# Masks of a third head group on TensorE, q and k of the second batch in four half-transfers, and a new order of steps

## The chip, the cores and the metric

The kernel runs on one core of one Trainium2 chip. Times are device microseconds of that core, one launch. A core has five engines with queues of their own: TensorE (PE; its weight loads are listed as PEld), VectorE (DVE), ScalarE (ACT), GpSimd (POOL) and SyncE (SP), and 16 DMA engines that the queues share. Matmul results land in eight banks of PSUM; a bank is free for the next matmul once another engine has read it.

## The reference

```python
# q, k, v: (8, 8, 576, 64); window 32
scores = (q @ k.T) / sqrt(64);  scores = where(|i - j| <= 32, scores, -1e9)
attn = softmax(scores);  a = attn @ v
x = a.transpose(0, 2, 1, 3).reshape(4608, 512)
# mixture of experts, 8 experts, top 1, w1 (8, 512, 1024), w2 (8, 1024, 512)
logits = x @ w_gate + modality_bias[modality_id]
e = argmax(logits);  gate = softmax(logits)[e]
out = gate * (relu(x @ w1[e]) @ w2[e])
```

## The kernel before, in words

The whole program is one list of steps written out by hand, the string ORDER. A step is a name with numbers, then the engine it goes to (`/v` DVE, `/a` ACT, `/p` POOL), or the PSUM banks it writes (`:0123`). A loop at the end of the function calls the function of each step in turn, and every engine runs its own instructions in that order; waits between engines come from the data. So the order of the list is the order of each engine's queue, and a step that waits holds up all that stands behind it on its engine.

Attention, per batch b (8) and head group g (2 per batch, four heads each; group number 2b + g):
- `l.b.u.g` loads q (u = 0) or k (u = 1) of batch b through POOL's DMA queue, cast to bf16; g = 2 takes both groups in one transfer (576 KB), g = 0 or 1 one group (288 KB). `lv.b.i` loads a half of v (288 KB).
- `t.b.g.u` transposes one of them on DVE into the layout for the scores.
- `SA`, `SB` are the score matmuls of a group in two parts, four banks each; `sa`, `sb` the exps on ACT into the tile pt (sa is one instruction, sb two).
- The band mask is applied in one of two ways. For groups listed in `PM`, `MA` and `MB` first write a table of 0 and a huge negative number into the banks (4 matmuls of 384 columns; MB has 4 of 128 columns more), and the scores add to it. For the others, `M.it` multiplies pt by a 0/1 mask on DVE, two steps of two heads for a group; `it` runs over 32 pairs of heads, so group 2 has M4 and M5.
- `V.it` is the product with v (18 matmuls, two banks), `v.it` the division by the sum and the write to x_t on DVE (a reciprocal, then one product).

Dispatch: `s0` to `s16` make, from the modality ids, each token's place in one list that holds the tokens of one modality from the front and those of the other from the back. `G.b` is a one-hot on DVE, `X.b.m` moves and transposes tokens with it on PE, `pa` and `pb` copy the result on ACT into XT. `Jo`, `Je` and `Jm` make the list of row numbers in the same way. `e` steps find the expert of each modality and the gate weights.

Experts: `W1.i` and `W2.i` load the weights of the expert of list end i (1024 KB each, POOL's queue). `U.t.mp` is 8 matmuls of 256 columns (a quarter of the first layer for 256 tokens, tile t), `u` the relu on ACT or DVE, `D.t.s.hf` 4 matmuls of 512 columns of the second layer, `y.t.s` the product with the gate weight, `O.t.s` the scatter of 128 rows to the output by POOL. Tile 18 is a short tile across the middle of the list. `L`, `lo`, `E`, `sm`, `rc` are the gate. `n2` and `n4` are fillers: 2 or 4 matmuls of 256 columns on zeros, whose result nobody reads. `K` steps make constants: Kw0 the zeros, Kw1 and Kw2 ones, Kn the table of the mask, Kb the 0/1 mask, Kq, Kp and Ko the padding of tiles, Kc others. Steps `c` check assumptions of this path; a general path stands behind an If at the end and is not run.

Steps around the change: U0.0 is the first expert matmul. It needs W1.0, `pa0.0` to `pa0.4`, and a free bank. The first D step needs W2.0.

## Time and profile before

| what | value |
|---|---|
| median of 3 runs | 209.55 us (209.44 to 210.11) |
| the profiled execution | 209.1 us, its span 207.5 us |
| PE, DVE, ACT, POOL busy | 194.9, 149.9, 133.0, 98.9 us |
| fillers on PE | 88 matmuls, 13.1 us busy |
| mean granted clock of TensorE | 0.996 of full speed |

The span is from the first to the last instruction; what the execution took beyond it (1.6 us) lies around the program. Busy times of matmuls overlap in the pipeline, so time per matmul is better read from the start of one group to the start of the next.

### The profile page before, as it was taken

To read this page: it belongs to the slowest core of one execution; us is meant where nothing else is said; L and a number is where in the kernel's file an instruction comes from. 1 tells how busy PE (TensorE), PEld (TensorE's weight loads), DVE (VectorE), ACT (ScalarE), POOL (GpSimd) and SP (SyncE) were. 2 spreads that over 40 slices of the span, in tenths; PEclk is the share of its full clock that TensorE was granted. 3 is DMA by queue.
4 is the path that set the end of the run, shared out by engine and by line. 5 is a ranking of instruction groups with operands and counts; after the bars stand their busy time and mean duration, and the time that the engine had idled before them with its cause. 6 is when DMAs were issued, how large, how long until landed. Compare 5 with 4: busy or idle time off the path is not lost. (4 is left out here: it accounts for less than half of the span.)

```text
span 207.5 us, 6240 instructions
## 1 busy us (share of the span) xinstructions
PE 194.9 (94%) x2585; PEld 139.8 (67%) x2585; DVE 149.9 (72%) x293; ACT 133.0 (64%) x226; POOL 98.9 (48%) x143
## 2 busy tenths in 40 slices
...
PEclk9999999999999999999999999999999999999998
...
GB/s 67 202 174 185 211 209 193 212 193 212 200 186 234 169 211 213 206 115 206 186 171 68 97 175 0 83 128 113 51 102 53 332 128 54 103 101 51 54 158 57
DMA packets 47629, 30.41 MB, mean 147 GB/s; under 512 B 38851, under 2 KB 38891, under 8 KB 47339
## 3 DMA queue, kind: packets, MB, share of 16 engines
...
## 5 line engine op out<-in xcount | busy, mean ns | idle before, releaser
L961 POOL DMA_INDIRECT out_dram<-ys,ids x37 | 40.6, 1098 | 87.2 <-ACT ys L952 33.8
L916 PE MATMUL banks<-XT,w_sb 128*128 128x256 bf16 x576 | 71.4, 273 | 0.3 <-DVE xt L758 0.3
L942 PE MATMUL banks<-w_sb,hT 128*128 128x512 bf16 x288 | 69.8, 379 | 0.0
L916 PEld LDWEIGHTS <-w_sb 128*128 128x128 bf16 x576 | 53.8, 98 | 10.9 <-issue 1.3
L695 ACT ACTIVATE pt<-banks 128x1536 bf16<-128x1536 f32 x32 | 46.4, 1453 | 14.0 <-PE banks L687 9.5
L933 ACT ACTIVATE hT<-banks 128x512 bf16<-128x512 f32 x57 | 33.0, 600 | 30.0 <-PE banks L916 27.5
L942 PEld LDWEIGHTS <-hT 128*128 128x128 bf16 x296 | 26.7, 98 | 25.6 <-issue 0.6
L655 DVE STREAM_TRANSPOSE qk<-qk 128x576 int32<-128x576 int32 x32 | 38.5, 1244 | 1.8 <-DMA qk<-in_q_dram 1.1
L712 DVE TENSOR_TENSOR pt<-pt,mask 128x1920 bf16<-128x1920 bf16 x28 | 32.1, 1169 | 3.5 <-ACT pt L695 3.4
L758 DVE TENSOR_TENSOR xt<-banks,recs 128x640 bf16<-128x640 f32 x32 | 26.4, 824 | 1.2
L729 PEld LDWEIGHTS <-pt 128*128 128x128 bf16 x576 | 21.2, 97 | 3.6 <-issue 0.4
L729 PE MATMUL banks<-vt,pt 128*128 128x65 bf16 x576 | 22.7, 193 | 0.4 <-DVE pt L712 0.2
L931 DVE TENSOR_SCALAR hT<-banks 128x512 bf16<-128x512 f32 x17 | 11.5, 685 | 15.9 <-PE banks L916 15.9
L952 ACT ACTIVATE ys<-banks,Gt 128x512 f32<-128x512 f32 x20 | 13.7, 691 | 12.9 <-PE banks L942 12.1
L798 ACT CAST XT<-banks 128x352 f32 (+3 forms) x40 | 18.0, 449 | 5.7 <-PE banks L778 4.9
L687 PE MATMUL banks<-qk 32*128 32x192 bf16 (+1 forms) x640 | 18.8, 239 | 2.5 <-DVE oh_ab L613 1.6
L231 POOL DMA_DIRECT2D vt<-in_v_dram x16 | 20.5, 1285 | 0.2 <-issue 0.2
L954 DVE TENSOR_SCALAR ys<-banks,Gt 128x512 f32<-128x512 f32 x17 | 12.7, 744 | 10.3 <-PE banks L942 4.7
L812 ACT CAST XT<-banks 128x352 f32 (+2 forms) x39 | 17.6, 452 | 1.9 <-PE banks L778 1.3
L687 PEld LDWEIGHTS <-qk 32*128 32x128 bf16 x640 | 12.3, 93 | 9.6 <-issue 6.8
L970 PE MATMUL banks<-zero_b 128*128 128x256 bf16 x88 | 13.1, 297 | 1.8 <-POOL zero_b L320 1.3
L778 PEld LDWEIGHTS <-xt 128*128 128x128 bf16 x160 | 10.5, 98 | 4.9 <-issue 0.8
...
## 6 DMA issues: line engine op xcount, KB each, us to landing
vt<-in_v_dram POOLq DMA_DIRECT2D x16, 288.0 KB
w_sb<-in_moe_w_dram POOLq DMA_DIRECT2D x4, 1024.0 KB
...
wx<-w_sb SPq DMA_DIRECT2D x2, 1024.0 KB, 6.2
out_dram<-ys,ids POOLq DMA_INDIRECT x37
qk<-in_k_dram POOLq DMA_DIRECT2D x2, 288.0 KB
qk<-in_q_dram POOLq DMA_DIRECT2D x2, 288.0 KB
```

Of the source, the lines that this page charges most:

```text
L231: nc.gpsimd.dma_start(v_t[b % NV][:, n_ * i:n_ * i + n_, 0:D], v[b].rearrange("h s d -> (h s) d").rearrange("(n p) d -> p n d", p=P)[:, n_ ...
L655: nc.vector.transpose(qk_t[b % 2][:, g, at:at + S].rearrange("p (t r) -> p r t", r=R), Ct["l", b][:, u, g].bitcast(I32).rearrange("p (r j) ...
L687: nc.tensor.matmul(st[:, h, WIN * i_:WIN * i_ + w_], qk[32 * h:32 * h + 32, c_, QK + k0:QK + k0 + P], qk[32 * h:32 * h + 32, c_, q0:q0 + w ...
L695: nc.scalar.activation(pt[:, :, 2 * part:2 * part + 2, 0:WIN], st[:, :, 0:2 * WIN].rearrange("p h (j c) -> p h j c", c=WIN), ACT.Exp, scal ...
L712: nc.vector.tensor_tensor(out=p_ap, in0=p_ap, in1=mask[:], op=ALU.mult)
L729: nc.tensor.matmul(o_ap, pt[:, c1:c1 + P], vt[:, g0 + j, 0:D + 1], start=(m == 0 and i_ == 0), stop=(i_ == len(mine) - 1), skip_group_chec ...
L758: nc.vector.tensor_tensor(out=o_ap, in0=o_v[:, :, :, 0:D], in1=rec.unsqueeze(3).to_broadcast([P, 2, NM, D]), op=ALU.mult)
L798: ins = nc.scalar.copy(XT[:, :, bass.ds(r_, w_)], Ct["X", b, m][:, :, 0:w_])
L916: ins = nc.tensor.matmul(ph[:, u_, :], w1[:, f0:f0 + 2 * P - 1:2], rhs, start=(kd == 0), stop=(kd == n_kd - 1))
L933: nc.scalar.activation(o_ap, i_ap, ACT.Relu)
L942: nc.tensor.matmul(Ct["D", t_, s_], Ct["h", t_][:, kf, P * s_:P * s_ + P], w2, start=(kf == 0), stop=(kf == n_kf - 1))
L961: ins = nc.gpsimd.indirect_dma_start(out=out, out_offset=bass.IndirectOffsetOnAxis(ap=ids[:, u_:u_ + 1], axis=0), in_=Ct["y", t_, s_][:], ...
```

## The change

- `PM` becomes (0,1,2): group 2, the first of batch 1, gets `MB1.0` and `MA1.0` on PE; `M4` and `M5` on DVE go.
- q and k of batch 1 come in four transfers of one group each, in the order k of group 0, q of group 0, then after v of batch 0 q of group 1, v's first half of batch 1, and k of group 1, instead of one transfer of q and, later, one of k.
- The order is new throughout. Steps change engine: Kw0, Kw1, Kw2, Kq1, s0, e9, Je1.2, Je7.2 go to DVE; Kv and e5 to POOL; relu and output steps are exchanged between ACT and DVE (u on DVE 19 instead of 17, y 16 instead of 17). There are 80 fillers instead of 88. In the new order U0.0 stands behind Jm0, and 8 fillers stand between U1.2 and D0.0.0.
- `y` gets a third way, "2", that splits the step between ACT and DVE. No step of the new order asks for it.

The diff, ORDER cut to its start and its end:

```diff
-Km Kh/v Ki Kw0/p l0.1.0/p n2.256:0 n2.256:0 l0.0.0/p Kq1/a n2.256:0 l0.0.1/p n2.256:0 Kg n4.256:0 Kj/p e0/v Kq0/v
-l0.1.1/p Kp0/v n2.256:0 l1.0.2/p n2.256:0 Kv/v Ke/v n4.256:0 Kw1/p Kn0/p Ko2/a Ko1/v e1/v Kp1/a e2/v n2.256:0 t0.0.1/v
-n2.256:0 Kw2/p Kn1/p n2.256:0 n2.256:0 e3/v n2.256:0 e4/v n2.256:0 t0.0.0/v n2.256:0 n2.256:0 MA0.0:0123 e6/v lv0.0/p
-Ko0/v Kb/v SA0.0 n2.256:4 MB0.0:4567 t0.1.0/v sa0.0/a lv0.1/p SB0.0 t0.1.1/v n2.256:0 Kc2/p MB0.1:0123 sb0.0/a e5/v
-Jy10/v l1.1.2/p SB0.1 Kc0/p sb0.1/a n2.256:4 t1.1.0/v s0/p n4.256:5 Kc4/p MA0.1:4567 t1.0.0/v SA0.1 e7/p lv1.0/p s1:1
-V0:23 sa0.1/a s2/v e8/v s3/v s4 n2.256:0 v0/v s5 W1.0/p s6/a V1:45 s8/v s7 V2:23 v1/v s9/a s10/a r0/a n2.256:6 Kc3/p
-n2.256:0 n2.256:7 v2/v n2.256:0 n4.256:4 W1.1/p n2.256:4 s11/v V3:12 t1.0.1/v Kc1/p n2.256:0 n4.256:7 s12/p Kc6/p v3/v
-SA1.0:4567 lv1.1/p n2.256:0 n4.256:0 s13/v sa1.0/a t1.1.1/v SB1.0:0123 W2.0/p s15/v s14/v sb1.0/a n2.256:4 s16/v
-l2.1.2/p n2.256:5 c0/v SB1.1:4567 G0/v Je1.0/v Je0.0/v sb1.1/a X0.0:3 M5/v Je0.1/p n4.256:1 l2.0.2/p X0.1:0 M4/v V5:12
-e9/p pa0.0/a X0.4:7 pb0.0/a v5/v Kc5/p pa0.1/a X0.2:3 V4:56 pb0.1/a Je1.1/p Jo0/v pa0.2/a n2.256:1 X0.3:4 pb0.2/a
-n4.256:2 Je1.2/p v4/v pa0.3/a SA1.1:0123 lv2.0/p pa0.4/a Jo1/v sa1.1/a U0.0:6 G1/v Je0.2/p U0.2:5 l3.0.2/p pb0.3/a M7/v
-u0.0/a Jm0:0 U0.1:1 pb0.4/a r2/a M6/v U1.2:6 u0.1/a Je2.0/v V7:23 Jy2/v Jx0/v u0.2/a Je3.0/v U1.3:1 Jo2/v r3/a Je3.1/p
-v7/v V6:45 Je3.2/p u1.2/a U1.0:0 Je2.1/p u1.3/a v6/v Je2.2/p U0.3:2 u1.0/a Jo3/v l3.1.2/p X1.0:5 X1.2:0 u0.3/a G2/v
-X1.3:4 X1.1:1 pb1.0/a Jm1:2 pb1.1/a L0:3 Je5.0/v D0.1.0:6 Jy1/v pb1.2/a Je4.0/v Je5.1/p c1/v pa1.0/a lo0/v Jo4/v Je4.1/p
-D0.1.1 E0/a pa1.1/a Je5.2/p sm0/v pa1.2/a Jx1/v D0.0.0:1 Jo5/v Je4.2/p pb1.3/a pa1.3/a t2.0.1/v W2.1/p X1.4:0 Jm2:3
-pb1.4/a D0.0.1 pa1.4/a rc0/v Je7.0/v y0.1/a Je6.0/v L1:5 Je7.1/p Jx2/v U3.2:0 lo1/v Je6.1/p t2.0.0/v U2.3:7 Je6.2/p
-u3.2/a lv2.1/p y0.0/a Jo6/v SB2.0:3456 u2.3/a Jo7/v U2.0:0 E1/a lv3.0/p sb2.0/a t2.1.1/v U2.1:7 Je7.2/p t2.1.0/v U2.2:1
-u2.0/a u2.1/a SA2.0:2345 t3.0.0/v l4.1.2/p u2.2/a Jm3:0 D2.0.0:7 sa2.0/a Jx3/v t3.1.0/v U1.1:0 M9/v SA2.1:1234 u1.1/a
...
-E9/a u16.2/a D16.0.0:6 u17.0/v c13/v D16.0.1 sm9/v rc9/v U17.3:1 y16.0/v D14.0.1 O16.0/p D14.1.0:6 D14.1.1 U17.1:3
-y14.1/a u17.3/a U18.1:2 O14.1/p y14.0/a U18.0:6 D16.1.0:1 u17.1/a u18.0/v D16.1.1 u18.1/v U17.2:6 y16.1/a c14:2
-D17.1.0:3 O16.1/p u17.2/a c15/v c16/a D17.1.1 O14.0/p D17.0.0:6 D17.0.1 y17.1/a D18.0.0:2 y17.0/v O17.1/p D18.0.1
-y18.0/a c17 O17.0/p O18.0/p
+Km Kh/v Kw0/v Kw1/v Ki l0.1.0/p n2.256:0 Kp1/v n2.256:0 l0.0.0/p Kp0/a Ko0/v Kq1/v n4.256:0 l0.0.1/p Kw2/v Kg n2.256:0
+Kj/p e0/v Kq0/v n2.256:0 l0.1.1/p Ke/v n4.256:0 l1.1.0/p n2.256:0 l1.0.0/p n2.256:0 t0.0.1/v Kn0/p n2.256:0 n4.256:0
+Kn1/p n2.256:0 n4.256:0 t0.0.0/v n2.256:0 n4.256:0 MA0.0:0123 e1/v e2/v t0.1.0/v SA0.0 lv0.0/p MB0.0:4567 sa0.0/a e3/v
+lv0.1/p SB0.0 t0.1.1/v Ko1/a n2.256:0 sb0.0/a Kc2/p MB0.1:0123 s0/v t1.0.1/v SB0.1 l1.0.1/p e6/v lv1.0/p Kb/v n2.256:4
+sb0.1/a n2.256:5 MA0.1:4567 t1.0.0/v Kc0/p SA0.1 Kc3/p sa0.1/a s1:0 n2.256:1 n2.256:2 s2/v e4/v V0:23 s3/v l1.1.1/p
+s11/v s4 s5 n2.256:1 W1.0/p v0/v s6/a V1:45 n4.256:6 s8/v s7 v1/v V3:23 s10/a s9/a V2:01 r0/a lv1.1/p v3/v MB1.0:4567
+v2/v Kc1/p SB1.0 s12/p e7/p n2.256:2 t1.1.0/v sb1.0/a MA1.0:0123 W1.1/p SA1.0 G0/v Kc4/p s13/v t1.1.1/v sa1.0/a Kc5/p
+n2.256:4 X0.2:4 X0.0:5 X0.1:7 n2.256:6 e8/v s15/v pa0.0/a s14/v SB1.1:0123 e9/v pb0.0/a s16/v pa0.1/a Je1.0/v n2.256:6
+Jo1/v V4:56 pb0.1/a Je1.1/p sb1.1/a n2.256:7 Je0.0/v n4.256:7 v4/v Je0.1/p n2.256:7 n2.256:7 X0.3:7 W2.0/p Jo0/v V5:56
+pa0.2/a Je0.2/p pb0.2/a X0.4:0 Je1.2/v v5/v pa0.3/a l2.0.2/p SA1.1:1234 pb0.3/a pa0.4/a G1/v Jm0:7 pb0.4/a U0.0:5
+sa1.1/a Jx0/v Jy10/v Je3.0/v Je2.0/v U0.1:7 Je3.1/p Jo3/v Je2.1/p U0.2:1 u0.0/v u0.1/a e5/p Je2.2/p M6/v U0.3:0 Je3.2/p
+L0:5 Jo2/v l2.1.2/p u0.3/a V6:67 u0.2/a M7/v Jm1:0 U1.0:2 Jx1/v v6/v V7:01 u1.0/a U1.3:3 Je4.0/v v7/v Je4.1/p U1.2:6
+u1.3/a Je5.0/v n2.256:3 Jy2/v lo0/v Je5.1/p X1.1:0 G2/v E0/a X1.0:2 u1.2/a X1.3:5 l3.0.2/p X1.2:1 pa1.0/a s17/v n2.256:7
+Jo4/v X1.4:6 n4.256:4 pa1.1/a Je5.2/p D0.0.0:3 Jo5/v pa1.2/a Je4.2/p pb1.0/a Kc6/p Jm2:4 pb1.1/a D0.1.0:2 Je6.0/v
+pa1.3/a l3.1.2/p sm0/v Jy1/v pb1.2/a c0/v D0.1.1 Jo6/v pa1.4/a pb1.3/a rc0/v Je7.0/v D0.0.1 pb1.4/a t2.1.0/v Je7.1/p
+y0.1/a U2.0:6 Je6.1/p r3/a t2.0.0/v lv2.0/p L1:2 u2.0/a U3.1:5 lo1/v t2.0.1/v E1/a y0.0/a W2.1/p U3.2:6 u3.1/a Je6.2/p
+sm1/v Ko2/a SB2.0:0123 rc1/v Je7.2/v u3.2/a lv2.1/p Jo7/v U2.1:5 sb2.0/a t2.1.1/v U2.2:6 Jx2/v l4.1.2/p Jm3:4 u2.1/a
+SA2.0:0123 Jx3/v u2.2/a Jy0/v U1.1:5 Jy4/v Jy3/v sa2.0/a c1/v Jy5/v Jy6/v U2.3:6 Jy7/v t3.0.1/v SA2.1:0123 u2.3/a Jy8/v
+D2.1.0:4 M9/v u1.1/a sa2.1/a D2.1.1 t3.0.0/v V9:56 y2.1/a SB2.1:0123 v9/v U3.3:4 sb2.1/a M8/v D2.0.0:5 Jy9/v t3.1.1/v
+D2.0.1 O0.0/p u3.3/a V8:67 M10/v l4.0.2/p SB3.0:0123 y2.0/a D1.1.0:4 M11/v O0.1/p sb3.0/a U3.0:5 v8/v Kv/p O2.0/p D1.1.1
+t3.1.0/v V10:01 lv3.1/p u3.0/a V11:23 v10/v r2/a D1.0.0:7 O2.1/p v11/v y1.1/a D1.0.1 r1/a lv3.0/p t4.0.1/v X2.0:2 X2.1:0
+X2.3:1 X2.4:6 pa2.0/a y1.0/v X2.2:3 lv4.0/p pb2.0/a D3.0.0:5 pa2.1/a G3/v pb2.1/a D3.0.1 G4/v pa2.2/a O1.0/p pb2.2/a
+D3.1.0:0 pa2.3/a pb2.3/a l5.0.2/p D3.1.1 y3.0/v pb2.4/a pa2.4/a t4.0.0/v SA3.0:1234 y3.1/a L2:5 sa3.0/a O3.1/p lo2/v
+U5.0:6 l5.1.2/p u5.0/a SB3.1:0123 M13/v O1.1/p U4.1:6 sb3.1/a t4.1.1/v U5.2:7 t4.1.0/v V13:45 E2/a u5.2/a sm2/v
+SA3.1:0123 c2/v u4.1/a l6.0.2/p v13/v U5.3:7 sa3.1/a O3.0/p M12/v U4.2:6 lv4.1/p U5.1:4 M15/v u5.3/a u4.2/a SB4.0:0123
+M14/v lv5.0/p u5.1/a V12:56 D5.0.0:4 sb4.0/a v12/v D5.0.1 rc2/v V14:56 y5.0/a U4.0:0 v14/v V15:12 u4.0/a SA4.1:3456
...
+u13.3/a sm6/v rc6/v pa7.0/a X7.2:1 D13.1.0:5 u12.3/a pb7.1/a D12.0.1 pa7.1/a pa7.2/a X7.3:7 D13.1.1 y12.0/v pa7.3/a c5/v
+pb7.2/a O12.0/p D10.1.0:4 c6/v pb7.3/a y13.1/v L7:0 pa7.4/a O13.1/p D12.1.0:2 xe/a lo7/v c7/v D13.0.0:6 c8/v D10.1.1
+L8:0 y10.1/a L9:5 D12.1.1 lo8/v lo9/v c9/v D13.0.1 c10/v y12.1/a c11/v U14.0:5 c12/v O12.1/p U14.3:4 O10.1/p U14.1:2
+u14.0/v U16.3:0 u14.1/a U16.1:1 u16.3/a c13/a E8/a U16.0:2 E7/a u16.1/a sm7/v u14.3/v U16.2:3 rc7/v u16.0/v N/p y13.0/v
+U14.2:4 u16.2/a E9/a D14.0.0:2 u14.2/v sm9/v U17.3:3 rc9/v sm8/v D14.1.0:4 u17.3/a D14.1.1 c14:3 D14.0.1 y14.1/a c15/v
+rc8/v D16.1.0:3 O14.1/p y14.0/a D16.0.0:4 O14.0/p U15.1:2 D16.1.1 U17.2:6 y16.1/v U15.3:1 O16.1/p u17.2/v u15.1/v
+U17.0:3 c16/v D16.0.1 u15.3/a u17.0/a U15.0:1 U17.1:3 u15.0/a U18.0:1 u17.1/a D15.0.0:2 y16.0/a D17.1.0:3 O16.0/p
+D17.0.0:4 O13.0/p D17.0.1 D17.1.1 U15.2:6 y17.1/v u18.0/v D15.1.0:0 O17.1/p u15.2/v U18.1:1 y17.0/v D15.0.1 u18.1/a
+O17.0/p D15.1.1 y15.0/v D18.0.0:1 y15.1/v O15.0/p D18.0.1 y18.0/a c17 O15.1/p O18.0/p
...
-    PM = (0,1)
+    PM = (0,1,2)
...
-        if eng == "a":
+        if eng == "2":
+            h_ = HD // 2
+            nc.scalar.activation(ys[:, 0:h_], Ct["D", t_, s_][:, 0:h_], ACT.Copy, scale=g_)
+            nc.vector.tensor_scalar(out=ys[:, h_:HD], in0=Ct["D", t_, s_][:, h_:HD], scalar1=g_, scalar2=None, op0=ALU.mult)
+        elif eng == "a":
             nc.scalar.activation(ys[:], Ct["D", t_, s_], ACT.Copy, scale=g_)
```

## Rows read from the trace of the kernel before

**Rows 1.** The page, parts 1 and 2: busy time of each engine (us, share of the span, instructions), and TensorE's granted clock in 40 equal slices of the span, in tenths of full speed.
```profile
PE 194.9 (94%) x2585; PEld 139.8 (67%) x2585; DVE 149.9 (72%) x293; ACT 133.0 (64%) x226; POOL 98.9 (48%) x143
...
PEclk9999999999999999999999999999999999999998
```

**Rows 2.** Busy time by stretch: from and to (us), length, busy us of each engine with its instructions, granted clock, mean share of the DMA engines, GB/s they moved.
```profile
20.00:30.00 10.00, 8.20 (x167) 6.55 (x166) 9.62 (x20) 7.15 (x11) 7.58 (x16) 1.00 1.29 207
30.00:40.00 10.00, 9.68 (x154) 8.60 (x151) 9.66 (x18) 7.37 (x14) 6.20 (x10) 1.00 1.38 202
...
40.27:201.30 161.03, 160.41 (x2043) 112.20 (x2040) 115.89 (x212) 106.68 (x184) 66.97 (x71) 1.00 0.80 142
```

**Rows 3.** The page, part 5, groups of instructions: line, engine, operation, tiles, count | busy us, mean ns of one | idle time before them and what ended most of it. The fillers n.
```profile
L970 PE MATMUL banks<-zero_b 128*128 128x256 bf16 x88 | 13.1, 297 | 1.8 <-POOL zero_b L320 1.3
```

**Rows 4.** Timeline of TensorE's matmuls up to the first D steps: start (us), time it took (us), engine, line, operation, tiles, count [idle time before and what ended it]. L970 are fillers, L664 and L668 the masks, L687 scores, L729 V, L778 X, L916 U, L537 Jm, L843 L, L942 D.
```profile
9.86 0.81 PE L664 MATMUL banks<-neg,ident 128*128 128x384 bf16 x4
...
10.83 0.64 PE L687 MATMUL banks<-qk 32*128 32x192 bf16 x24
...
18.74 1.69 PE L970 MATMUL banks<-zero_b 128*128 128x256 bf16 x14
20.27 0.71 PE L729 MATMUL banks<-vt,pt 128*128 128x65 bf16 x18
...
31.15 1.91 PE L916 MATMUL banks<-XT,w_sb 128*128 128x256 bf16 x16 [0.32 <-DVE xt L758]
32.89 0.49 PE L537 MATMUL banks<-ev,ohp 128*128 128x72 bf16 x10
33.21 1.04 PE L916 MATMUL banks<-XT,w_sb 128*128 128x256 bf16 x8
...
39.87 0.55 PE L843 MATMUL banks<-wgd,XT 128*128 128x8 bf16 x16
40.27 2.78 PE L942 MATMUL banks<-w_sb,hT 128*128 128x512 bf16 x12
42.89 0.33 PE L778 MATMUL banks<-oh,xt 128*128 128x96 bf16 x4
43.64 0.49 PE L537 MATMUL banks<-ev,ohp 128*128 128x72 bf16 x10 [0.42 <-POOL ev L529]
```

**Rows 5.** Timeline of VectorE from the first transpose of q and k to U0.0; columns as in rows 4. L655 are the transposes t, L429 the mask Kb, L743 and L758 a v step, L523 Je, L712 M, L507 Jo or G.
```profile
5.89 1.26 DVE L655 STREAM_TRANSPOSE qk<-qk 128x576 int32<-128x576 int32 x1 [0.39 <-DMA qk<-in_k_dram]
...
7.87 1.26 DVE L655 STREAM_TRANSPOSE qk<-qk 128x576 int32<-128x576 int32 x1 [0.49 <-DMA qk<-in_q_dram]
...
9.07 0.76 DVE L429 TENSOR_SCALAR mask<-neg 128x768 bf16<-128x768 bf16 x1
...
10.90 2.32 DVE L655 STREAM_TRANSPOSE qk<-qk 128x576 int32<-128x576 int32 x2
...
13.91 2.34 DVE L655 STREAM_TRANSPOSE qk<-qk 128x576 int32<-128x576 int32 x2 [0.64 <-DMA qk<-in_q_dram]
...
19.09 0.21 DVE L743 RECIPROCAL recs<-banks 128x10 f32<-128x10 f32 x1
...
20.07 0.19 DVE L487 SCALAR_TENSOR_TENSOR nbk<-Am,K 128x40 f32<-128x40 bf16 x1
20.52 1.25 DVE L655 STREAM_TRANSPOSE qk<-qk 128x576 int32<-128x576 int32 x1 [0.26 <-DMA qk<-in_k_dram]
...
25.27 0.59 DVE L523 TENSOR_TENSOR ev<-iob,pmd 128x180 bf16<-128x180 bf16 x2
25.79 2.51 DVE L712 TENSOR_TENSOR pt<-pt,mask 128x1920 bf16<-128x1920 bf16 x2
...
29.20 0.81 DVE L507 TENSOR_TENSOR ohp<-iob,pmd 128x640 bf16<-128x640 bf16 x1
29.93 0.21 DVE L743 RECIPROCAL recs<-banks 128x10 f32<-128x10 f32 x1
```

**Rows 6.** Timeline of ScalarE in the same stretch. L695 and L698 are the exps sa and sb, L798 and L812 the copies pa and pb.
```profile
22.46 2.79 ACT L695 ACTIVATE pt<-banks 128x1536 bf16<-128x1536 f32 x2 [3.89 <-PE banks L687]
25.14 0.60 ACT L698 ACTIVATE pt<-banks 128x512 bf16<-128x512 f32 x1
...
27.42 0.45 ACT L798 CAST XT<-banks 128x288 bf16<-128x288 f32 x1
...
28.70 0.56 ACT L798 CAST XT<-banks 128x352 f32 x1
```

**Rows 7.** Timeline of GpSimd (POOL) at the start. L215 issues loads of q and k, L647 W2.0, L526 is a Je step.
```profile
0.93 0.31 POOL L320 MEMSET zero_b<- 128x256 bf16 x1 [0.29 <-POOLq L1228]
1.51 0.71 POOL L215 DMA_DIRECT2D qk<-in_k_dram  x1 [0.27 <-issue]
...
22.81 0.76 POOL L647 DMA_DIRECT2D w_sb<-in_moe_w_dram  x1
...
25.95 1.33 POOL L526 TENSOR_TENSOR ev<-ev,hi__105 128x180 bf16<-128x180 bf16 x1 [1.69 <-DVE ev L523]
```

**Rows 8.** The page, part 6, DMA issues: tensors, queue, operation, count, KB each (at the destination).
```profile
vt<-in_v_dram POOLq DMA_DIRECT2D x16, 288.0 KB
w_sb<-in_moe_w_dram POOLq DMA_DIRECT2D x4, 1024.0 KB
```

**Rows 9.** Timeline of the end, all engines: the last scatter, of y18.
```profile
202.43 0.97 POOL L961 DMA_INDIRECT out_dram<-ys,ids  x1 [0.63 <-ACTq L1211]
```

54 lines of the change are left out of this document (20 added, 34 removed).

## Prediction

> **What bounds the kernel now.** I read the page's busy shares first: TensorE (PE) is busy 94% of the span and its clock is granted in full throughout [rows 1], so no clock loss is to be won back. Busy time of pipelined matmuls says little about density, so next came the busy time by stretch [rows 2] and the start times of PE's groups [rows 3, 4]. The reader is to see two regimes. Before U0.0 at 31.15, PE has little to do and the order feeds it fillers: 88 in all, 13.1 us by busy time [rows 3], 14 of them alone between 18.74 and 20.27 [rows 4], which is 0.109 us each. From U0.0 on, PE is dense: 16 U matmuls from 31.15 to 32.89, 12 D matmuls from 40.27 to 42.89 [rows 4], which is 0.87 us for a U or a D step; from 40.27 to 201.30 PE is busy 160.41 of 161.03 us [rows 2]. So the end is set by when the dense stream starts and by what is added to it; an engine that is faster later on gives nothing.
>
> The start, then, is VectorE (DVE) and the loads. DVE is busy 9.62 and 9.66 us of 10 in the two stretches from 20 to 40 [rows 2]. It waits for transfers at 5.89, 7.87, 13.91 and 20.52 [rows 5]. The last is k of batch 1, and ScalarE's exps of batch 1 sit idle 3.89 us until 22.46 for it [rows 6]. U0.0 itself, at 31.15, is released by a DVE evacuation, a v step (xt, L758) [rows 4].
>
> **How early the first k half lands.** The second half-transfer (288 KB) has its transpose at 7.87, and the one that reads q of batch 1, four halves' worth further, at 13.91 [rows 5]: 1.51 us a half. The new order queues k of head group 0 as the fifth half: 7.87 + 3 x 1.51 = 12.4. POOL's first DMA is issued at 1.51 behind the zero_b memset of 0.31 us [rows 7], which moves to DVE: 0.3 us earlier (bounds 0 and 0.58, from 0.93 to 1.51). Taken: 12.1. Here a rule speaks against the change: the Trainium skill, "DMA: Bandwidth & Descriptors", section "Anatomy of one DMA", gives every POOL-issued DMA a fixed cost of some 2.0 us beside its bytes. The row's 1.51 us for a whole half does not agree with a cost paid in series; if the two extra transfers paid it so, W2.0 would land 4 us later, at 42.5 instead of 38.5 (below).
> From rows, the price of an extra transfer is bounded by nothing below and by 1.98 - 1.51 = 0.47 us above (the half from 5.89 to 7.87 against the mean), 0.94 us for two. The two added issues cost POOL 0.7 us each [rows 7], long before the queue runs dry.
>
> **The DVE chain to U0.0.** From that transpose on I find no idle DVE, so it is a sum, in the new order, up to the end of v5, which frees bank 5 for U0.0:
> - four transposes of batch 1, 1.16 us each (two from 10.90 to 13.22 [rows 5]): 4.64
> - Kb, the mask: 9.07 to 10.90 [rows 5]: 1.83
> - six v steps, 0.98 each (19.09 to 20.07 [rows 5]): 5.88
> - G0 and two Jo, 0.73 each (29.20 to 29.93 [rows 5]): 2.19
> - two Je, 0.26 each (25.27 to 25.79 [rows 5]): 0.52
> - fourteen small steps (e6 s2 e4 s3 s11 s8 s13 e8 s15 s14 e9 twice, s16 Je1.2), some 0.14 each. The nearest row is one of 0.19 us (20.07) that is overlapped by its neighbours; bounds 0.1 and 0.2: 2.0 (1.4 to 2.8).
>
> 12.1 + 17.1 = 29.2, so U0.0 at 29.25 instead of 31.15. What was on this chain and is gone: M5 and M4, 2.5 us (from 25.79), and the 0.64 and 0.26 us of waiting at 13.91 and 20.52. What is new on it: s0, e9 and Je1.2 from POOL, e4, the zero_b, one_f and ones memsets (those lie before 5.89, where DVE waits anyway).
>
> ScalarE must keep up: sa1.0 would end at about 24.1 (it needs v2, then the masks and scores of MA1.0 and SA1.0), four copies at 0.32 each (27.42 to 28.70), sb1.1 (1.40 and 0.60) and five copies [rows 6] put pa0.4 near 29.1. So two conditions meet within 0.2 us; I take the later.
>
> **The masks on PE.** MB1.0 and MA1.0 cost 0.97 us (9.86 to 10.83, both kinds of mask matmul) and at most 0.81 (the four wide ones at 9.86) [rows 4]. They lie at about 19 to 22, where PE runs fillers today (from 18.74 [rows 4]), so they cost nothing; were that cover gone, 1.8 us. The fillers ahead of U0.0 go from 88 to 72, and 8 come after it.
>
> **From U0.0 to the first D.** Before: 40.27 - 31.15 = 9.12. The new order does the same steps, less Jm0 (0.32, 32.89 to 33.21 [rows 4], now ahead of U0.0), plus 8 fillers (0.87): 9.67. X1.4 also moves ahead of the first D; it is done in both orders, so I leave it out of both sides. PE is no longer always the last to be ready: V6 waits for M6, Jm1 for Jo2, V7 for M7 and X1 for v7, all on DVE. The same kind of sum from v5 on (G1, Jo3, Jo2; three Je; M6 and M7 at 2.51 for two; v6, v7; u0.0 and three small ones, some 1.0 together: 8.4 us) ends v7 at 37.6, and X1, the fillers and D0 follow: I take 0.43 us of stalls in all (bounds 0 and 1.3). D0.0.0: 29.25 + 9.67 + 0.43 = 39.35, and break-even is 40.27. Two loads could forbid it. W1.1 now stands behind one v half more: k of batch 1 had landed at 20.52, W1.1's end is 2624 KB further, at 204.5 GB/s (mean of 207 and 202 [rows 2]) 13.1 us, so 33.4 to 34 against a need near 34.3 in that sum (U1.0). W2.0 keeps its place, 3648 KB after k by the sizes of the transfers [rows 8]: 18.3 us, 38.8, or 38.5 with the earlier first issue, against 39.35. So W2.0 caps the gain at 40.27 - 38.5 = 1.8 us, whatever DVE does.
>
> **After it.** 161 us of dense PE, the same matmuls. Jm2 stalls today on POOL's Je (0.42 us at 43.64 [rows 4]); it will again (0 to 0.7, taken 0.4): no difference. SB3.1 takes the banks of SA3.0 only L2 (0.40, 39.87 to 40.27 [rows 4]) and one U (0.87) later, 1.3 us, while an exp of 1.4 us [rows 6] must lie between, itself behind y3.1 on ScalarE: 0.4 us lost, against two like stalls that before has further on, which the new order may or may not keep: +0.05 in sum (bounds -0.6 and +1.2). The exchanged engines of u and y are even in number within two, in the dense part, where PE covers them; uncovered, a u or y late by its own length would be late by at most one U step, 0.87 us. The end keeps its form: last D, y18, its scatter at 202.43, 0.97 us of POOL [rows 9]; O15.1 is now just ahead of O18 on POOL, and its own 0.97 us ends about when y18 does: 0 (bounds 0 and +0.6). The "2" branch of y is called by no step of the order: nothing.
>
> Sum: 39.35 - 40.27 + 0.05 = -0.9 us. The profiled execution took 209.1 us (span 207.5), so 208.2; the median of the runs is 209.55, so 208.65, told as 208.7.
>
> **Rivals.**
> 1. The gain is spent before D0. DVE stays the bound up to v7, and its steps on two SBUF tensors may run slow beside POOL's Je, as M5 and M4 did, 2.51 us for two [rows 5], while POOL's Je from 25.95 took 1.33 [rows 7]. Three per cent more on these 25 us puts v7 at 38.3 and D0.0.0 at 40.0 to 40.3: 209.2 to 209.6. For it: DVE has no slack there today. Against: without M5 and M4 fewer such steps are left.
> 2. Slower: t1.0.1 blocks the head of DVE's queue. It now stands before Kb, t1.0.0 and s2, and behind s2 wait the whole dispatch (s4 to s16), and v0, which frees banks for PE. If the k half lands with the q half after it (the transfers share the same engines), at 13.6 to 13.9, every step is 1.5 to 1.8 us late: 210.1 to 210.5. The gain is gone when it lands after 13.0. For it: the wait at 13.91 shows the sixth half only. Against: earlier halves landed one by one, 5.89 and 7.87.
> 3. Slower: POOL issues W2.0 late. It stands behind Je1.1 and Je0.1, which wait for pmd on DVE, where today it is issued at 22.81, ahead of Je [rows 7]. Two Je of 1.33 us behind the Je of DVE put the issue at 28.1. The first half took 5.89 - 1.51 = 4.4 us from issue to use, 1.5 of it for its bytes; 1024 KB at 204.5 GB/s are 5.1, so W2.0 lands 8.0 us after its issue at the soonest. From an issue at 31.5 on, each us is a us of D0 and of the end; at 34, D0 comes at 42.0: 211.3. Against: DVE would have to be 3.4 us later than the sum.
> 4. Slower: each transfer holds up the queue. At the 0.47 us above, W2.0 comes at 39.4, just hidden: 208.7 again. If instead the queue paid what the lone first half took beyond its issue and its bytes (4.4 - 0.7 - 1.5 = 2.2 us [rows 5, 7]) for each extra transfer, W2.0 would land at 42.9 and D0 2.6 us past break-even: 212.1. It decides from 0.9 us a transfer. Against: 1.51 us a half over three transfers, which leaves no room for it. The 2.0 us of the skill's page named above would make it 211.7.
>
> **How the numbers follow.** My forecast 0.47, rival 1 0.29, rival 2 0.13, rival 3 0.06, rival 4 (its dear form) 0.05. About 0.3% (0.6 us) is what a measurement of this kernel can tell from no change, so faster 0.47, same 0.29, slower 0.24. The forecast's own range is 207.7 to 208.95: the cap of W2.0 with 0.05 kept, to the sum's upper bounds. The range for all reaches into rival 2: 207.6 to 210.3.
>
> **What would show it.** Right: the k half's transpose at 12.1 (not 13.6), no DVE wait for a transfer between it and v5, ScalarE's idle of 3.89 us gone, U0.0 near 29.3, first D near 39.5, and the last matmul as much earlier as the first D. Wrong at the chain: U0.0 past 30.6. Wrong at the loads: a first D released by the w transfer. Wrong after it: a dense stretch from the first D longer than 161 us.

## The result: 0.8% slower

| | kernel before | kernel after |
|---|---|---|
| median of 21 runs each, taken in turn | 209.82 us (209.06 to 211.34) | 211.50 us (209.73 to 212.27) |
| ratio, 95% interval | | 1.0079 [1.0062, 1.0096] |
| profiled execution, span | 209.1, 207.5 us | 211.72, 210.1 us |

208.7 us was predicted, with a range of 207.6 to 210.3. The time lies above that range, and above the kernel before, where a gain was forecast. In the tables the ratios leave out three slow executions (214.16 and 214.21 us of a2, 253.61 us of b4), while the medians count them.

**Where the time went.** The profiled spans differ by 2.6 us (the medians by 1.7: the execution profiled before was 0.7 us below its median, the one after 0.2 above). Four points of TensorE's stream divide the difference, each the start of a group of matmuls: U0.0, SB2.0 (the first scores of batch 2), D18.0.1 (the last group) and the end.

| stretch | before | after | difference |
|---|---|---|---|
| start to U0.0 | 31.15 | 30.07 | -1.08 |
| U0.0 to SB2.0 | 15.92 | 18.94 | +3.02 |
| SB2.0 to D18.0.1 | 153.33 | 153.15 | -0.18 |
| D18.0.1 to the end | 7.10 | 7.96 | +0.86 |

So the head of the kernel did become faster, and what lost was the 19 us behind it and, by less, the end. With the price of each step from start to start (U 0.87, D 0.86, V 0.55, Jm 0.32, L 0.40, X 0.17 to 0.22, a filler 0.109), the second stretch of before is 15.20 us of steps and 0.73 of waits; of after 15.75 of steps (one U more, one Jm less), 0.87 of fillers and 2.33 of waits. The U that moved ahead of SB2.0 is missing behind it, so 0.55 of the 3.02 us is only shifted and 2.47 is lost. The third stretch has 0.55 us less to do and is just 0.18 shorter; among its waits in after are that of SB3.1 (0.45) and that of V13 for a half of v (0.55), while the longest before is 0.37.

The page's first part, after, answers to [rows 1]: TensorE is as full as before.

```profile
PE 194.7 (93%) x2568; PEld 140.8 (67%) x2589; DVE 150.0 (71%) x298; ACT 132.6 (63%) x223; POOL 98.5 (47%) x141
```

TensorE of the kernel after, timeline around V0 and at U0.0 (start us, us, engine, line, operation, tiles, shape, count, in brackets the idle time before and what ended it; the view of the last line ends inside its group):

```profile
16.37 0.71 PE L728 MATMUL banks<-vt,pt 128*128 128x65 bf16 x18 [1.00 <-DMA vt<-in_v_dram]
...
30.07 3.11 PE L915 MATMUL banks<-XT,w_sb 128*128 128x256 bf16 x27
```

V0 waits 1.00 us for the first half of v of batch 0. U0.0 answers to 31.15 of [rows 4]. VectorE of after, from the k half to v0:

```profile
12.16 1.26 DVE L654 STREAM_TRANSPOSE qk<-qk 128x576 int32<-128x576 int32 x1 [0.22 <-DMA qk<-in_k_dram]
13.27 0.17 DVE L612 TENSOR_TENSOR oh_ab<-e,ext_e 128x16 f32<-128x16 f32 x1
13.29 1.52 DVE L428 TENSOR_SCALAR mask<-neg 128x768 bf16<-128x768 bf16 x3
14.73 1.24 DVE L654 STREAM_TRANSPOSE qk<-qk 128x576 int32<-128x576 int32 x1
...
17.11 0.22 DVE L742 RECIPROCAL recs<-banks 128x10 f32<-128x10 f32 x1 [0.68 <-PE banks L728]
```

The k half's transpose is at 12.16, no transpose waits after it (compare 13.91 and 20.52 in [rows 5]), and the one idle time, 0.68 us, is V0's wait handed on. Now the stretch that lost, on TensorE:

```profile
33.96 0.71 PE L728 MATMUL banks<-vt,pt 128*128 128x65 bf16 x18
35.93 0.71 PE L536 MATMUL banks<-ev,ohp 128*128 128x72 bf16 x10 [1.26 <-POOL ev L528]
...
41.53 1.03 PE L941 MATMUL banks<-w_sb,hT 128*128 128x512 bf16 x3
42.98 0.48 PE L536 MATMUL banks<-ev,ohp 128*128 128x72 bf16 x10 [0.42 <-POOL ev L528]
...
47.17 1.91 PE L915 MATMUL banks<-XT,w_sb 128*128 128x256 bf16 x16
49.01 0.64 PE L686 MATMUL banks<-qk 32*128 32x192 bf16 x24
```

V6 starts at 33.96 and takes 0.55, but Jm1 comes at 35.93: 1.42 us lost, released by POOL (line 528 is Je.2). Its second half waits 0.23 us more, for Je3.2. Jm2 at 42.98 loses 0.59, the same as before (42.89 and 43.64 in [rows 4]). The first D is at 41.53 (40.27 before). Two U from 47.17 end at 48.92, and SB2.0 follows at 49.01, seemingly without a wait. POOL of after, at Jm1:

```profile
32.81 1.13 POOL L610 TENSOR_TENSOR mbd<-mb_bc,pm__132 128x16 f32<-128x16 f32 x1
33.92 2.35 POOL L528 TENSOR_SCALAR ev<-ev,pr 128x180 bf16<-128x180 bf16 x2
```

POOL works on mbd (step e5, which the change moved to POOL), then on Je2.2 (33.92 to 35.88) and Je3.2; they end at 36.27. In the kernel before, POOL did Je2.2 and Je3.2 when VectorE's M6 and M7 were over (they end at 34.82), and beside Je4.2 and Je5.2 VectorE did two Jo:

```profile
36.78 0.42 POOL L529 TENSOR_SCALAR ev<-ev,pr 128x180 bf16<-128x180 bf16 x1
...
37.75 0.42 POOL L529 TENSOR_SCALAR ev<-ev,pr 128x180 bf16<-128x180 bf16 x1
...
41.65 1.95 POOL L529 TENSOR_SCALAR ev<-ev,pr 128x180 bf16<-128x180 bf16 x2
```

So the same step took 0.42 us there, 0.98 beside the two Jo, and 1.96 in after beside Jo2 and M7. VectorE of after beside it:

```profile
32.57 1.29 DVE L711 TENSOR_TENSOR pt<-pt,mask 128x1920 bf16<-128x1920 bf16 x1
33.78 0.83 DVE L506 TENSOR_TENSOR ohp<-iob,pmd 128x640 bf16<-128x640 bf16 x1
34.54 1.14 DVE L711 TENSOR_TENSOR pt<-pt,mask 128x1920 bf16<-128x1920 bf16 x1
36.74 0.23 DVE L546 TENSOR_TENSOR hl<-hl,banks 128x72 f32<-128x72 f32 x1 [1.06 <-issue]
```

VectorE does M6, Jo2 and M7, which ends at 35.68, and then idles 1.06 us, because Jx1, which reads the result of Jm1, stands next in its queue (line 546), ahead of v6. And VectorE of after ahead of SB2.0:

```profile
45.22 2.33 DVE L654 STREAM_TRANSPOSE qk<-qk 128x576 int32<-128x576 int32 x2
47.42 0.19 DVE L853 TENSOR_TENSOR lo__146<-banks,mbd 128x32 f32<-128x32 f32 x1
47.53 1.25 DVE L654 STREAM_TRANSPOSE qk<-qk 128x576 int32<-128x576 int32 x1
```

These are t2.1.0, t2.0.0 and, last, t2.0.1. SB2.0 needs the last two. They end at 48.78, 0.14 us before TensorE is there: a second bound lay hidden right under the first. The last scatter of after, on POOL, against 202.43 in [rows 9]:

```profile
204.27 0.97 POOL L964 DMA_INDIRECT out_dram<-ys,ids  x1 [0.31 <-ACT ys L955]
```

It comes 2.1 us behind D18.0.1, as before (2.03); the rest of the 0.86 us lies behind its issue, 5.85 us to the end instead of 5.07. Three scatters stand close ahead of it here.

### The profile page after: what moved, and what is told of

Read it like the earlier page. It is cut to its first block, busy times and chain, and to the rows that moved or that the text cites. A ratio compares the mean times of both kernels' runs of the same rounds, so it can differ in the third digit from the quotient of the medians.

```text
span 210.1 us, 6219 instructions
## 1 busy us (share of the span) xinstructions
PE 194.7 (93%) x2568; PEld 140.8 (67%) x2589; DVE 150.0 (71%) x298; ACT 132.6 (63%) x223; POOL 98.5 (47%) x141
## 5 line engine op out<-in xcount | busy, mean ns | idle before, releaser
L964 POOL DMA_INDIRECT out_dram<-ys,ids x37 | 39.5, 1069 | 89.6 <-ACT ys L955 47.0
L915 PE MATMUL banks<-XT,w_sb 128*128 128x256 bf16 x576 | 69.5, 273 | 0.1
L941 PE MATMUL banks<-w_sb,hT 128*128 128x512 bf16 x267 | 67.1, 379 | 1.2 <-issue 0.2
L915 PEld LDWEIGHTS <-w_sb 128*128 128x128 bf16 x576 | 54.4, 98 | 9.8 <-issue 1.0
L932 ACT ACTIVATE hT<-banks 128x512 bf16<-128x512 f32 x55 | 31.9, 597 | 35.5 <-PE banks L915 35.4
L654 DVE STREAM_TRANSPOSE qk<-qk 128x576 int32<-128x576 int32 x32 | 39.1, 1247 | 3.1 <-DMA qk<-in_k_dram 2.5
L711 DVE TENSOR_TENSOR pt<-pt,mask 128x1920 bf16<-128x1920 bf16 x26 | 29.4, 1154 | 2.4 <-ACT pt L694 2.2
L957 DVE TENSOR_SCALAR ys<-banks,Gt 128x512 f32<-128x512 f32 x16 | 11.9, 744 | 16.7 <-PE banks L941 7.9
L930 DVE TENSOR_SCALAR hT<-banks 128x512 bf16<-128x512 f32 x19 | 12.8, 685 | 4.2 <-PE banks L915 4.0
L742 DVE RECIPROCAL recs<-banks 128x10 f32<-128x10 f32 x32 | 6.8, 214 | 8.5 <-PE banks L728 6.8
```

Source lines behind the costliest of these rows:

```text
L654: nc.vector.transpose(qk_t[b % 2][:, g, at:at + S].rearrange("p (t r) -> p r t", r=R), Ct["l", b][:, u, g].bitcast(I32).rearrange("p (r j) ...
L711: nc.vector.tensor_tensor(out=p_ap, in0=p_ap, in1=mask[:], op=ALU.mult)
L915: ins = nc.tensor.matmul(ph[:, u_, :], w1[:, f0:f0 + 2 * P - 1:2], rhs, start=(kd == 0), stop=(kd == n_kd - 1))
L932: nc.scalar.activation(o_ap, i_ap, ACT.Relu)
L941: nc.tensor.matmul(Ct["D", t_, s_], Ct["h", t_][:, kf, P * s_:P * s_ + P], w2, start=(kf == 0), stop=(kf == n_kf - 1))
L964: ins = nc.gpsimd.indirect_dma_start(out=out, out_offset=bass.IndirectOffsetOnAxis(ap=ids[:, u_:u_ + 1], axis=0), in_=Ct["y", t_, s_][:], ...
```

## Experiments

Each ratio is to the kernel before, measured beside it on the same chip, with its 95% interval; it is not the quotient of two medians, and the medians are not all from one chip. "First D", "SB2.0" and the last group are starts on TensorE in each profile. Line numbers of the test kernels are one higher than those of after.

| kernel | median us | ratio | U0.0 | first D | SB2.0 | D18.0.1 |
|---|---|---|---|---|---|---|
| before | 209.45 to 210.29 beside these | 1 | 31.15 | 40.27 | 47.07 | 200.40 |
| after | 211.50 | 1.0079 [1.0062, 1.0096] | 30.07 | 41.53 | 49.01 | 202.16 |
| a1 mbd on VectorE | 211.37 | 1.0064 [1.0036, 1.0092] | 30.16 | 41.45 | 48.93 | 201.63 |
| a2 v ahead of q | 212.03 | 1.0063 [1.0022, 1.0104] | 32.69 | 44.16 | 51.65 | 204.36 |
| a3 no late fillers | 211.07 | 1.0049 [1.0020, 1.0077] | 29.46 | 40.10 | 48.42 | 201.12 |
| a4 tail | 211.19 | 1.0041 [1.0016, 1.0066] | 29.44 | 40.91 | 48.39 | 201.03 |
| b1 halves alone | 209.70 | 1.0025 [0.9994, 1.0057] | 31.19 | 40.32 | 47.12 | 200.22 |
| b2 masks alone | 210.02 | 1.0023 [0.9998, 1.0047] | 31.67 | 40.79 | 47.59 | 200.42 |
| b3 halves and masks | 210.20 | 1.0037 [1.0007, 1.0067] | 32.66 | 41.79 | 48.59 | 201.42 |
| b4 scores early | 209.47 | 0.9982 [0.9962, 1.0003] | 31.11 | 40.24 | 47.04 | 200.15 |
| d4 the same, fillers in another bank | 209.90 | 0.9984 [0.9951, 1.0018] | 31.08 | 40.20 | 47.01 | 200.14 |
| c1 Jm later | 211.64 | 1.0090 [1.0066, 1.0114] | 30.24 | 40.61 | 48.66 | 201.68 |
| d2 transposes alone | 212.50 | 1.0079 [1.0043, 1.0114] | 29.71 | 41.18 | 48.66 | 202.30 |
| d1 Jm and transposes | 210.22 | 0.9974 [0.9942, 1.0005] | 29.50 | 40.12 | 47.17 | 200.37 |
| c2 Jm, fillers, lv3, tail | 210.68 | 1.0041 [1.0022, 1.0061] | 29.29 | 39.74 | 48.22 | 201.18 |
| d3 all of these | 209.82 | 0.9965 [0.9935, 0.9995] | 30.24 | 40.17 | 47.06 | 200.09 |

U0.0 moves by up to 0.95 us between executions of kernels with after's head (29.29 to 30.24, a2 left out): V0 starts at 15.55 to 15.75 in some and at 16.00 to 16.55 in others, and U0.0 follows V0 by 13.69 to 13.75 us in all nine. So in this order U0.0 hangs on V0, which in the late ones waits for the first half of v (1.00 us in after). Times inside one profile are therefore compared from V6 or U0.0 on.

**a1.** One step to another engine:

```diff
- u0.1/a e5/p Je2.2/p M6/v
+ sb0.0/a e5/v ...   u0.1/a Je2.2/p M6/v
```

> The kernel after, with one step moved back: the subtraction that makes mbd (e5) runs on VectorE behind sb0.0's place in the order, as before, and not on POOL between Je2.1 and Je2.2. Theory A (POOL's Je chain sets Jm1, and with it v6, v7 and the first D): Je2.2 starts about 1.1 us earlier, Jm1 comes at 34.7 to 35.0 instead of 35.93 (Jo2's end at 34.61 is the next bound), the first D 0.9 to 1.1 us earlier than 41.53, the time 0.7 to 1.1 us below the kernel after, so 210.4 to 210.8. Theory B (the gain is given back at Jm2, which waits for POOL too, or PE would have waited anyway for v7): first D earlier by under 0.3 us, or Jm2's wait longer by what was won; the time within 0.3 us of the kernel after.

POOL of a1, then its TensorE:

```profile
33.04 3.14 POOL L529 TENSOR_SCALAR ev<-ev,pr 128x180 bf16<-128x180 bf16 x2
```

```profile
34.95 0.32 PE L537 MATMUL banks<-ev,ohp 128*128 128x72 bf16 x5 [0.18 <-POOL ev L529]
36.23 0.32 PE L537 MATMUL banks<-ev,ohp 128*128 128x72 bf16 x5 [0.96 <-POOL ev L529]
```

Je2.2 did start earlier, 33.04 for 33.92, but the two Je took 3.14 us (1.86 and 1.30) where the same two took 2.35 in after, and the second half of Jm1 came at 36.23. Theory A missed. Theory B's numbers came (the first D 0.08 us earlier, the time that of after), but not for its reason: POOL, with 1.13 us of work taken off it, ended 0.09 us earlier (36.18 for 36.27), again just behind VectorE's M7 (35.90 here). From V6 to the first D it took 7.39 us, in after 7.57.

**a2.**

```diff
- l1.1.0/p n2.256:0 l1.0.0/p ...   lv0.0/p
+ l1.1.0/p lv0.0/p n2.256:0 l1.0.0/p
```

> The kernel after, with the first half of batch 0's v (lv0.0) queued between the two first halves of batch 1 (behind k's, ahead of q's) instead of behind both. Theory A (V0 waits about 1 us for this transfer, and everything to U0.0 hangs on V0): it lands 1.5 us earlier, V0 starts at 15.4 to 15.7 instead of 16.37, VectorE's idle 0.68 us at 17.11 goes, U0.0 comes at 29.3 to 29.6 instead of 30.07, the time is 0.5 to 0.7 us lower. Theory B (U0.0 hangs on ScalarE and its exps, or the transpose of the q half, now 1.5 us later, takes the place): U0.0 within 0.2 us of 30.07, the time within 0.3 us of the kernel after.

VectorE of a2, then its TensorE (an execution of 214.16 us, 2.1 us above this kernel's median, so its sizes are not typical):

```profile
16.93 1.26 DVE L655 STREAM_TRANSPOSE qk<-qk 128x576 int32<-128x576 int32 x1 [2.05 <-DMA qk<-in_q_dram]
```

```profile
15.67 0.71 PE L729 MATMUL banks<-vt,pt 128*128 128x65 bf16 x18
18.27 0.30 PE L471 MATMUL banks<-ones,Am 128*40 128x128 bf16 x1 [1.89 <-DVE sp_i L609]
```

V0 came at 15.67, as theory A said, and in this execution nothing was won: the q half landed some 3 us later (its transpose is at 16.93, in after at 14.73, where it had landed at 13.62), the transpose held VectorE for 2.05 us, and the whole dispatch stood behind it. There it is the prediction's second rival, brought about by one transfer. Whether other executions of a2 go the same way is not shown: the interval of its ratio holds both after's ratio and one that is lower by theory A's 0.5 to 0.7 us.

**a3.**

```diff
- n2.256:3 ... n2.256:7 ... n4.256:4     (between U1.2 and D0.0.0)
```

> The kernel after without the 8 filler matmuls that stand between U1.3 and the first D; nothing else is changed. Theory A (they cost what they last, since PE is dense from U0.0 on): 8 x 0.109 = 0.87 us less. Theory B (they stand where PE would wait anyway: Jm2 right behind the first D waits for POOL's Je4.2, which ends at 42.93 whatever PE does): the first D up to 0.87 us earlier, Jm2 at the same 43 us, its wait longer by as much, the time within 0.3 us of the kernel after.

TensorE of a3:

```profile
40.10 1.03 PE L942 MATMUL banks<-w_sb,hT 128*128 128x512 bf16 x3
42.39 0.48 PE L537 MATMUL banks<-ev,ohp 128*128 128x72 bf16 x10 [1.27 <-POOL ev L529]
```

The profile shows theory B: from V6 to the first D it took 6.74 us instead of 7.57, and Jm2's wait, from start to start, was 1.43 instead of 0.59. U0.0 to SB2.0 is 18.95 us, as in after. The time alone does not decide: its ratio lies between the two theories, and its interval overlaps that of after.

**a4.** The last steps spaced (other steps left out):

```diff
- D17.0.1 D17.1.1 U15.2:6 D15.1.0:0 U18.1:1 y17.0/v D15.0.1 D15.1.1 D18.0.0:1 D18.0.1
+ D17.0.1 U15.2:6 y17.0/a D17.1.1 U18.1:1 D15.0.1 D15.1.0:0 D15.1.1 D18.0.0:1 D18.0.1
```

> The kernel after with another order of the last steps: D17.0 and D17.1 are finished ahead of D15's second halves, y17.0 is made by ScalarE, D15.0 is finished before D15.1, so that the last four scatters come free 0.9 to 1.7 us apart and not in a pile. Theory A (the pile behind y17.0 costs the time after PE's end): the end comes 6.3 to 6.5 us after PE's last matmul instead of 7.1, the time is 0.5 to 0.8 us lower. Theory B (the end is y18 and its own scatter whatever is ahead of it): the time within 0.3 us of the kernel after.

From D18.0.1 to the end: 7.04 to 8.75 us in the six kernels with after's tail (mean 8.18, a2 left out), 7.53 to 7.77 in the three with this one (7.63), 7.09 to 7.75 in the six with before's (7.48). That favours theory A at 0.55 us; but the six times with after's tail spread over 1.7 us, and the intervals of after and a4 touch, so it is not shown.

**b1, b2, b3.** The parts alone, in the order of before: the transfers renamed in place and the transposes in their order; MA1.0 and MB1.0 right ahead of SA1.0 and SB1.0.

```diff
- l1.0.2/p ... l1.1.2/p ... t1.1.0/v ... t1.0.0/v ... t1.0.1/v ... t1.1.1/v
+ l1.1.0/p l1.0.0/p ... l1.0.1/p l1.1.1/p ... t1.0.1/v ... t1.0.0/v ... t1.1.0/v ... t1.1.1/v
- PM = (0,1)     SA1.0:4567 ... SB1.0:0123 ... M5/v ... M4/v
+ PM = (0,1,2)   MA1.0:4567 SA1.0 ... MB1.0:0123 SB1.0
```

> The kernel before with one part of the change alone: q and k of batch 1 come in four transfers by halves, k and q of the first head group in the place of the whole q, the other two in the place of the whole k; its transposes are taken in the order of landing (k, q of group 0, then q, k of group 1). Theory A (the prediction's chain): VectorE's waits of 0.64 and 0.26 us go, sa1.0 starts 1 to 2 us before 22.46, U0.0 comes about 0.9 us before 31.15, the time is 0.5 to 0.9 us below the kernel before. Theory B (VectorE's later work, the two mask products above all, sets U0.0 and the waits only shift): U0.0 within 0.3 us of 31.15, the time within 0.3 us of before. Theory C (each added transfer holds up the queue): W2.0 and the first D later, the time 0.9 us or more above.

> The kernel before with another part alone: the masks of the third head group are added on TensorE (MA1.0 and MB1.0 right ahead of its scores) and VectorE's two mask products M4 and M5 (2.51 us at 25.79) are gone; the order is otherwise that of before. Theory A: v5 and v4 come 1.5 to 2.5 us earlier on VectorE, U0.0 at 28.7 to 29.7, W2.0 (about 38.5) caps what the first D wins at 1.8 us: the time 1.0 to 1.8 us below before. Theory B (ScalarE's exps of the group, which end near 26.3, or POOL's Je chain come next, or the gain goes into waits before the first D): the time within 0.3 to 0.5 us of before.

> The kernel before with both parts, halves and masks, in the order of before, so that of the change only the new order is missing. Theory A (the two parts pay, the new order loses it): the time 1.2 to 1.8 us below before, the first D near 38.6 and released by W2.0. Theory B (the parts themselves cannot move the first D, because POOL's and VectorE's steps behind U0.0 set it): U0.0 1.5 us or more earlier, the first D within 0.4 us of 40.27, the time within 0.4 us of before.

ScalarE's first two exps of batch 1 in b2 (sa1.0 and sb1.0), and VectorE's first v step of that batch:

```profile
22.46 1.45 ACT L695 ACTIVATE pt<-banks 128x1536 bf16<-128x1536 f32 x1 [4.27 <-DVE xt L758]
24.66 1.45 ACT L695 ACTIVATE pt<-banks 128x1536 bf16<-128x1536 f32 x1 [0.75 <-PE banks L687]
```

```profile
28.72 0.22 DVE L743 RECIPROCAL recs<-banks 128x10 f32<-128x10 f32 x1 [3.24 <-ACT XT L798]
```

The same two in b3:

```profile
23.44 1.45 ACT L695 ACTIVATE pt<-banks 128x1536 bf16<-128x1536 f32 x1 [4.27 <-PE banks L687]
25.65 1.45 ACT L695 ACTIVATE pt<-banks 128x1536 bf16<-128x1536 f32 x1 [0.76 <-PE banks L687]
```

```profile
29.71 0.22 DVE L743 RECIPROCAL recs<-banks 128x10 f32<-128x10 f32 x1 [3.71 <-ACT XT L798]
```

b1 and b2 came out as theory B, b3 as neither: both its theories had U0.0 or the first D no later than before, and U0.0 came 1.5 us later, the first D too, the time 0.37% above. With halves alone the waits only shift: the two of 0.64 and 0.26 us are gone, but VectorE now idles 0.72 us ahead of 16.49, for a matmul that waits for an exp of batch 0, and sa1.0 (22.51; 22.46 in [rows 6]) and U0.0 stay. With the masks, where M5 and M4 were, VectorE idles 3.24 and 3.71 us until ScalarE is through its exps and the first copy. In the four kernels with masks in the order of before (b2, b3, b4, d4) U0.0 follows sb1.0 (24.66, 25.65, 24.06 and 23.98) by 7.01 to 7.10 us: there ScalarE's work from sb1.0 on sets U0.0, not VectorE's. And in b2 and b3 ScalarE idles 0.75 us ahead of sb1.0, because the mask matmuls MB1.0 (0.97 us of TensorE) now stand ahead of SB1.0. With both parts, MA1.0 (0.74 us) and SA1.0 also stand behind 20 fillers in TensorE's queue, and U0.0 comes 1.5 us later (0.6 of it from V0, late in that execution: 16.68 for 16.06).

**b4, d4.** 14 fillers for the first scores:

```diff
- V2:23 ... (14 fillers) ... V3:12 ... MA1.0:4567 SA1.0
+ V2:23 ... MA1.0:4567 v2/v SA1.0 ... V3:12
```

> The kernel before with halves and masks, and with one more edit: 14 fillers behind V2 are out, and MA1.0 and SA1.0 (mask and first scores of batch 1) stand in their place, ahead of V3 and not behind it and 20 fillers. Theory A (in the order of before the two parts win nothing since ScalarE's first exp of batch 1 hangs on TensorE's in-order queue, fillers included: sa1.0 at 22.46, 22.51, 22.46 and 23.44 in the kernel before, with halves, with masks, with both): sa1.0 starts at 20.5 to 21.5, U0.0 at 30.0 to 31.3 instead of 32.66 with both, the time 1 to 2 us below the run with both. Theory B (VectorE's v steps set sa1.0 whatever stands on TensorE): sa1.0 within 0.5 us of 23.44, the time within 0.3 us of the run with both.

> The kernel before with halves, masks and the early MA1.0 and SA1.0 in the place of 14 fillers, and all later fillers ahead of sa1.0 in bank 0, so that none touches the banks of SA1.0. (In the run before this one they were in bank 7: they overwrote a part of the scores of one head, changing values, and sa1.0 waited for them until 21.95.) Theory A (sa1.0 is the head of ScalarE's chain to U0.0): sa1.0 at 20.5 to 20.9, U0.0 0.5 us or more before 31.11. Theory B (SB1.0, whose banks come free with v3 near 22.4, is the head): sb1.0 at 24.0 to 24.1 again, U0.0 within 0.2 us of 31.1, the time within 0.3 us of 209.5.

ScalarE of d4:

```profile
20.57 1.45 ACT L695 ACTIVATE pt<-banks 128x1536 bf16<-128x1536 f32 x1 [1.85 <-PE banks L687]
23.98 1.45 ACT L695 ACTIVATE pt<-banks 128x1536 bf16<-128x1536 f32 x1 [1.96 <-DVE pmd L169]
```

In b4 the fillers behind SA1.0 write to bank 7, one of its four, and overwrite a part of its scores, so b4 does not compute what the others do; d4 has them in bank 0. The first exp moved from 23.44 to 21.95 (b4, where it waits for those fillers) and 20.57 (d4), U0.0 to 31.11 and 31.08: of the last 1.4 us nothing arrived, since SB1.0, whose banks come free with v3, is next (sb1.0 at 23.98). Against b3 the ratio is 0.55% lower, the 1 to 2 us of b4's theory A, while d4 came out as theory B. Without the fillers ahead of SA1.0 the two parts show neither a cost nor a gain: both intervals hold 1.

**c1, d2, d1.** Jm1 and Jm2 moved (with Jx1, v7, Je6.0 and rc0, which stand beside them), then the transposes, then both:

```diff
- V6:67 ... Jm1:0 U1.0:2 Jx1/v v6/v V7:01 u1.0/a U1.3:3     D0.0.0:3 ... Jm2:4 ... D0.1.0:2 Je6.0/v ... D0.1.1
+ V6:67 ... U1.0:2 v6/v u1.0/a U1.3:3 V7:01 v7/v Jm1:4 Jx1/v     D0.0.0:3 ... D0.1.0:2 ... D0.1.1 Jm2:4 Je6.0/v
- t2.1.0/v ... t2.0.0/v ... lo1/v t2.0.1/v
+ t2.0.0/v ... lo1/v t2.0.1/v t2.1.0/v                      (d2)
+ Jy1/v t2.0.0/v ... Je7.0/v t2.0.1/v c0/v ... lo1/v t2.1.0/v   (d1)
```

> The kernel after with two products moved back in TensorE's order, nothing else: Jm1 stands behind U1.0, U1.3 and V7 (in bank 4) instead of ahead of them, Jm2 behind D0.1.1 instead of ahead of D0.1.0. In the profiles so far POOL's Je2.2 and Je3.2 end when VectorE's M7 does, 36.27 (after) and 36.13 (with mbd on VectorE, where the two last 3.14 us). Theory A (PE loses what it waits for POOL's Je, 1.42 us at Jm1 and 0.59 at Jm2): U1.0 starts right behind V6, no wait over 0.3 us at Jm1 or Jm2, from V6 to the first D 6.3 to 6.7 us instead of 7.5 to 7.6, the time 1.2 to 1.8 us below the kernel after (209.7 to 210.3). Theory B (V7 waits for M7 anyway, and the first D for v7 or for W2.0): V7 within 0.3 us of where it is, the first D too; only Jm2's 0.6 us is won. Theory C (the later Jm push Jm3 and what hangs on it): a new wait of 1 us or more behind 45 us.

> The kernel after with t2.1.0 behind t2.0.1 and nothing else. Theory A (in the kernel after SB2.0 is reached by TensorE at the same time as its transposes are done, so neither alone pays): the time within 0.3 us of the kernel after. Theory B (the transposes alone are the loss): SB2.0 1 us earlier, the time 0.8 us or more lower.

> The kernel after with Jm1 and Jm2 moved back (as in the run with that alone) and VectorE's transposes of batch 2 in another order: t2.0.0 in the idle time ahead of Je6.0, t2.0.1 right behind Je7.0, t2.1.0 last of the three, instead of t2.1.0, t2.0.0, t2.0.1. Theory A (SB2.0 is held by the last of the two transposes that it needs, which stood third): no wait over 0.3 us ahead of SB2.0, which comes 1.0 to 1.4 us earlier against V6 than in the kernel after (15.05 us behind V6 there, 13.5 to 14.0 here), the time 1.0 to 1.6 us below the kernel after. Theory B (the k transfer of batch 2, landing at 44.65, or its wait behind W2.0, holds SB2.0): SB2.0 not before 48 us, the time within 0.4 us of the kernel after.

TensorE of c1 at SB2.0, and VectorE's t2.0.1 ahead of it:

```profile
45.82 1.91 PE L916 MATMUL banks<-XT,w_sb 128*128 128x256 bf16 x16
48.66 0.64 PE L687 MATMUL banks<-qk 32*128 32x192 bf16 x24 [0.94 <-DVE sm L867]
```

```profile
47.36 1.24 DVE L655 STREAM_TRANSPOSE qk<-qk 128x576 int32<-128x576 int32 x1
```

VectorE's t2.0.0 and t2.0.1 in d1, and its SB2.0:

```profile
41.87 1.26 DVE L655 STREAM_TRANSPOSE qk<-qk 128x576 int32<-128x576 int32 x1 [0.32 <-DMA qk<-in_q_dram]
...
45.10 1.25 DVE L655 STREAM_TRANSPOSE qk<-qk 128x576 int32<-128x576 int32 x1 [0.29 <-DMA qk<-in_k_dram]
```

```profile
47.17 0.76 PE L687 MATMUL banks<-qk 32*128 32x192 bf16 x24
```

In c1 Jm1 and Jm2 do not wait, and the first D comes 6.47 us behind V6 (7.57 in after): theory A up to there. Then TensorE is at SB2.0 at 47.56 and waits for t2.0.1, which ends at 48.60 (the view names sm, which ends at the same time and which SB2.0 does not read): theory C, at 47 us and not by Jm3. The time is after's. With the transposes alone (d2) the time is after's too. With both (d1) SB2.0 comes 13.78 us behind V6 (15.05 in after) without a wait, and the ratio is 1% below after's. The two changes to the order are worth nothing alone and 2 us together. (d1 moves t2.0.0, t2.0.1 and c0 further ahead than d2, so the square is not exact: these places were not run with Jm1 and Jm2 where they were. In after TensorE is at SB2.0 at 48.92 in any case, 0.1 us ahead of its start.) t2.0.1 now waits for the k transfer itself and ends at 46.35; SB2.0, at 47.17, is TensorE's own time.

**c2, d3.** c1 with no late fillers, lv3.0 ahead of lv3.1 (V13's wait) and a4's tail; d3 adds d1's transposes and D0.1.0 in bank 7.

> The run above with three more edits to the kernel after: the 8 fillers ahead of the first D are out, lv3.0 is queued before lv3.1 (V13 waited 0.55 us for it), and the last steps have the order that spaces the scatters. Theory A (all of the 2 us are waits and fillers of the order, in series): the first D at 39.0 to 39.4, now just behind W2.0 (39.02), no wait at V13, the time 2.6 to 3.4 us below the kernel after, 208.1 to 208.9, so below the kernel before too. Theory B (the first D hangs on something else, W2.0 or v7, and the removed fillers come back as a wait): 0.8 us or less below the run above.

> The first run of these four with the fillers ahead of the first D out, D0.1.0 in bank 7 (bank 2 waited 0.8 us for ScalarE's copies), lv3.0 ahead of lv3.1 and the spaced tail. Theory A (the waits from U0.0 to SB2.0, the fillers and the tail are the whole loss): SB2.0 at 46.3 to 47.0, the time 2.0 to 2.8 us below the kernel after, 208.7 to 209.5, so at or below the kernel before. Theory B (W1.1 at 34.1 and W2.0 at 39.0 hold what is won): SB2.0 later than 47.3, the time 210 or more.

c2 fits neither of its theories: its first D, 39.74, is later than A's, and its time is 0.5% below c1's where B had 0.8 us at most. It wins 0.4% of after's 0.8, no more than a4 with its tail alone: SB2.0 waits 1.09 us as in c1, U1.0 now waits for the w transfer (0.34 us idle) and D0.1.0 for ScalarE's copies (0.60 from start to start, 0.43 idle). d3 is below before, by 0.35% [0.05, 0.65]: theory A's size, on the executions measured. From d1 (0.9974) it is not told apart, so what its further edits are worth is not shown. Its SB2.0, 47.06, is that of before (47.07) and a little past the 47.0 expected, with V0 late in that execution (16.55).

## Why the prediction was wrong, point by point

In the profiled pair the four parts of the sum came out so: up to U0.0 -1.08 us where -1.90 was forecast, from U0.0 to the first D +2.34 for +0.98, from the first D to D18.0.1 +0.50 for +0.05, the end +0.86 for 0. Every part missed to the same side; the second missed by most.

- **The k half at 12.1**: it landed at 12.14, but by two errors that cancel. The first issue came 0.04 us earlier (1.47 for 1.51 in [rows 7]) and not 0.3. The second half landed at 7.11, 0.7 us ahead of the 7.87 that the sum starts from, and the three halves behind it took 5.03 us and not 3 x 1.51 = 4.53. The number is right by luck.
- **The chain to v5, 17.1 us**: measured 29.92 - 12.16 = 17.76, of which 0.68 idle, so 17.08 of work. No transfer held VectorE in it, as forecast, and ScalarE's idle time ahead of its first exp of batch 1 fell from 3.89 to 2.43 us. What the sum lacked is V0's wait for the first v half, for which it had no row. U0.0 came at 30.07 instead of 29.25; where V0 was earlier (15.69 in a4), at 29.44.
- **From U0.0 to the first D, 9.67 + 0.43**: the step that failed. 11.46 us were measured, of which 1.65 are waits of Jm1 for POOL, where 0.43 was taken and 1.3 was the bound; another 0.17 is X1.4, which moved ahead of the first D and which the sum left out. The sum said that Jm1 waits for Jo2 "on DVE" and priced POOL's Je2.2 and Je3.2 nowhere, nor e5, which the change put in front of them; POOL ended at 36.27, Jo2 at 34.61. By a1 it is not e5 that mattered, but that POOL's Je now stand beside M6, Jo2 and M7. VectorE's own sum was right: from v5 to v7 (39.25) it worked 8.27 us, 8.4 forecast, and idled 1.06 behind Jm1.
- **After the first D, +0.05**: +0.50 was measured, inside the bounds. Jm2's wait was the same in both, as taken; SB3.1's was 0.45 for 0.4 taken; V13's 0.55 had no term. But the account stopped at the first D as if what follows were dense. The next point where several queues meet, SB2.0, was not looked at, and a3 and c1 show that an earlier first D is not kept there: SB2.0 follows U0.0 by 18.95 and 18.42 us in them, 18.94 in after.
- **The tail, 0**: +0.86 in these two executions and +0.70 in the mean over the kernels with either tail, above the bound of 0.6.
- **The range**: its upper end was said to follow from the sum's upper bounds, but 208.95 does not. The bounds of the stalls, of what comes after and of the tail alone (1.3 for 0.43, 1.2 for 0.05, 0.6 for 0) add up to 2.6 us above 208.65, so 211.3. The range was narrower than its own terms allow.
- **Rivals**: 1 had the place right and the mechanism the wrong way round: POOL slowed beside VectorE, while M6 and M7 took 2.43 us together (1.29 and 1.14) and 2.44 before. Its price, first D at 40.0 to 40.3, was too low. 2 did not happen in after (12.14), but something like it did in the one execution of a2. 3 and 4 did not: W2.0 was issued at 27.39 and landed at 39.02, and nothing waited for it; the halves landed at 10.63, 12.14 and 13.62. The dear form of 4 gave 211.7 to 212.1, close to the 211.50 measured, by a mechanism that is not there: the time alone would have spoken for it. The Trainium skill's fixed cost ("DMA: Bandwidth & Descriptors", "Anatomy of one DMA") does not show as one in series here: the steps are 1.51 and 1.48 us.
- **The masks at nothing**: nothing speaks against it in after's order, where VectorE was busy without a break from V0's end to v5, which frees U0.0's bank; it was not run apart. In before's order, b2 shows MB1.0 ahead of SB1.0 as 0.75 us of waiting, and b3 what happens when the cover is a filler ahead in the same queue: the filler is work there too.

What stays open: why the first half of v lands late in some executions, so that V0 comes up to 1.0 us later, and how much of the median's 1.7 us is the tail.
